# Writing transposed k and q in the order of their blocks, and loading v to match in eight transfers a chunk, in an attention and feed-forward kernel

## The chip, the cores and the metric

The kernel runs on one core of a Trainium2 chip. The time is the device time of one execution in microseconds (us). Several executions are taken, and each is marked fast, slow or unknown; only fast runs are compared. The profile is of one execution, and its span is some 2 us shorter than the time of that execution (564.6 and 566.4 us for the kernel before).

Short names: PE is TensorE (matmuls), PEld its weight loads, DVE is VectorE, ACT is ScalarE, POOL is GpSimd, SP is SyncE, which here only issues transfers, in order. L294 is line 294 of the kernel that the profile belongs to, so the same statement has another number in another kernel. An evacuation is the copy by which another engine takes a finished product away from TensorE. An issue is the instruction that starts a transfer; the transfer lands later.

## The reference, cut

```python
# q, k, v: (4, 8, 768, 48), alpha the same, in 0.8 to 1.0; all fp32
for t in range(S):
    state = alpha[:, :, t, :, None] * state + np.einsum('bhd,bhe->bhde', k[:, :, t], v[:, :, t])
    y[:, :, t] = np.einsum('bhd,bhde->bhe', q[:, :, t], state)
x = y.transpose(0, 2, 1, 3).reshape(3072, 384)
h = x @ w_in                                   # (384, 2048)
g = h * np.clip(h + 3.0, 0.0, 6.0) / 6.0
out = g @ w_out                                # (2048, 384)
```

## The kernel before, as far as the change touches it

The sequence is worked in 24 chunks of 128 tokens; two chunks are one group of 256 rows of the feed-forward part. Chunks 0 to 5 are loaded by token and transposed by TensorE. From chunk 6 on (`FIRST`), alpha, k and q come from DRAM with partition u holding tokens 4u to 4u+3, and VectorE turns them in blocks of 32 by 32. What leaves a block transpose is in the order (v, u), v being the token's place within its four. The kernel before writes it back in token order, each element 16 bytes after the last.

```python
def load_v(j, z):                              # by token, two transfers a chunk
    to = v_t[j].rearrange("s (p a) e -> s p a e", a=2)
    sv = rows(v, j).rearrange("(p a) s d -> s p a d", a=2)
    nc.sync.dma_start(out=to[:, :, 0, 0:D], in_=sv[:, :, 0])
    nc.sync.dma_start(out=to[:, :, 1, 64 - D : 64], in_=sv[:, :, 1])

def by_blocks(to, name, j):                    # k, q and alpha from chunk 6 on
    nc.vector.transpose(out=to.rearrange("r p (u v) -> r p v u", v=V),
                        in_=quads[name, j % NQ][:, :, :, 0:BLK])

def scaled(name, j):                           # k times R, q times P (decays along the chunk)
    ...
    by = R_t[j][:, :, 1:W] if name == "k" else without_first(P_t.pop(j))
    nc.vector.tensor_tensor(out=t, in0=src, in1=by, op=ALU.mult)

def write_k(j):                                # scaled k, turned again, goes to DRAM as far ...
    for o in range(V):
        nc.sync.dma_start(out=to[o], in_=src[BLK * o : BLK * (o + 1)])

def read_k(j):                                 # ... and is read back as kb, by token
    nc.sync.dma_start(out=kb_t[j].rearrange("s p r -> s (p r)"), in_=...)

def update(j):                                 # TensorE: state += kb^T v
    ...
def store2(g, i):                              # a finished quarter of a group's output
    nc.scalar.dma_start(out=out[j * C : (j + 1) * C, col * HD : (col + 1) * HD],
                        in_=oh_t.pop((g, i)))
```

All loads and k's round trip (`far`, then `kb`) are issued by SyncE, one after another; the stores are issued by ScalarE. A hand-made string of words fixes the order of all work on every engine: `lv.6.1` is the load of v for chunk 6, `kw.6` and `kr.6` are the two halves of k's round trip.

## Time and profile before

| | before |
|---|---|
| median of the first runs | 568.94 us (568.49 to 569.09) |
| span of the profiled run | 564.6 us |
| TensorE busy | 553.4 us, 98% |
| VectorE busy | 470.0 us, 83% |

The busy line, the stretches, TensorE's waits and the transposes are in the prediction below. Two views also belong here. The first is the chain of work that ended last, by engine, from the page:

```profile
PE 89%; DMA 6%; DVE 2%; SPq 1%; issue 0%; ACT 0%; DVEq 0%; ACTq 0%
```

The chain runs through TensorE for 89% of the span: that is a kernel bound by TensorE. The second is what SyncE's queue waited for (engine, line, what it waited for: us in all, times, longest us):

```profile
SPq L267 <- DMA out_dram<-oh: 27.7, 13, 4.6
SPq L267 <- DMA kb<-far: 9.0, 4, 3.1
```

L267 is a load of alpha, k or q. It waits, 13 times, for a *store* of results (`out_dram<-oh`), although no buffer connects the two.

### The profile page before, as it was taken

What the parts mean: (1) busy time and instruction counts of PE and PEld (TensorE: products, weight loads), DVE (VectorE), ACT (ScalarE), POOL (GpSimd) and SP (SyncE); (2) the same over time, 40 slices, a digit from 0 to 9 for tenths busy, and PEclk for the clock granted to TensorE, in tenths of its full rate; (3) what the DMA queues carried; (4) which work ended last, traced back from release to release, by engine and by line L of the source; (5) the groups of instructions that cost most, each with busy time, mean ns of one, the idle gap of its engine ahead of it and who ended that gap; (6) DMA issues with size and microseconds to landing.
All of it is one profiled execution on the core that took longest, in us unless ns stands there. A gap on an engine that the chain in (4) does not pass through costs nothing.

```text
span 564.6 us, 12762 instructions
## 1 busy us (share of the span) xinstructions
PE 553.4 (98%) x5236; PEld 513.2 (91%) x5236; DVE 470.0 (83%) x798; ACT 196.4 (35%) x348; POOL 56.0 (10%) x70
## 2 busy tenths in 40 slices
PE   8899999999899999999999999999999999999997
PEld 7688987599799989999999999999999999999997
DVE  7866997999899999998998978976999967754580
ACT  1457664112332332322422422432521422432420
POOL 2333435200001000100000000000000000000000
PEclk9979999999999999999999999999999999999999
DMA  9999677103533636264264353153154340000000
GB/s 147 188 186 168 186 230 196 52 16 63 139 90 87 145 71 155 54 139 90 60 148 107 77 121 85 20 146 78 45 129 94 83 122 8 1 22 8 1 30 21
DMA packets 121272, 53.73 MB, mean 95 GB/s; under 512 B 80638, under 2 KB 114174, under 8 KB 121214
## 3 DMA queue, kind: packets, MB, share of 16 engines
q1 hardware_dynamic: 114588, 48.19, 40.8%
q10 hardware_dynamic: 6624, 4.72, 2.5%
q8 instruction: 41, 0.67, 0.5%
q14 instruction: 19, 0.14, 0.1%
HBM read 44.24 MB, written 8.65 MB: 94 GB/s over the span
## 4 chain that ended last, share of the span: by engine, by line
PE 89%; DMA 6%; DVE 2%; SPq 1%; issue 0%; ACT 0%; DVEq 0%; ACTq 0%
PE m_ps L692 35%; PE m_ps L592 29%; PE m_ps L471 6%; PE sc_ps L346 4%; PE m_ps L509 4%; PE y_ps L440 4%; DMA rings<-in_k_dram 3%; PE y_ps L450 2%; PE m_ps L482 2%; DMA t<-in_v_dram 2%; PE u_ps L410 2%; DMA kb<-far 1%; PE tk_ps L288 1%; DMA far<-kq 1%; PE m_ps L524 0%
## 5 line engine op out<-in xcount | busy, mean ns | idle before, releaser
L692 PE MATMUL m_ps<-w,g_sb 128*128 128x192 f32 x704 | 121.2, 328 | 0.0
L692 PEld LDWEIGHTS m_ps<-w,g_sb 128*128 128x128 f32 x704 | 113.8, 190 | 2.3 <-issue 1.4
L598 ACT COPY g_sb<-m_ps 128x512 f32<-128x512 f32 x110 | 64.3, 584 | 138.3 <-PE m_ps L592 123.9
L692 PE MATMUL m_ps<-rings,g_sb 128*128 128x192 f32 x528 | 91.2, 326 | 0.0
L692 PEld LDWEIGHTS m_ps<-rings,g_sb 128*128 128x128 f32 x528 | 85.7, 190 | 0.0
L592 PE MATMUL m_ps<-xc,w 128*128 128x128 f32 x640 | 83.2, 278 | 0.2 <-ACT g_sb L598 0.2
L592 PEld LDWEIGHTS m_ps<-xc,w 128*128 128x128 f32 x640 | 77.2, 192 | 3.3 <-issue 1.4
L487 ACT ACTIVATE r<-g_sb,half 128x512 f32<-128x512 f32 x80 | 55.5, 719 | 57.0 <-DVE g_sb L529 22.8
L491 DVE SCALAR_TENSOR_TENSOR g_sb<-r,g_sb 128x512 f32<-128x512 f32 x80 | 54.5, 700 | 8.1 <-PE m_ps L692 4.8
L397 POOL TENSOR_TENSOR t<-t,R 128x384 f32<-128x384 f32 x20 | 20.9, 1043 | 383.8 <-DVE t L425 206.0
L592 PE MATMUL m_ps<-xT,raw 128*128 128x128 f32 x400 | 51.8, 276 | 0.0
L592 PEld LDWEIGHTS m_ps<-xT,raw 128*128 128x128 f32 x400 | 48.7, 192 | 0.3
L529 DVE TENSOR_TENSOR g_sb<-m_ps,g_sb 128x512 f32<-128x512 f32 x30 | 20.5, 686 | 27.2 <-ACT g_sb L598 26.5
L592 PE MATMUL m_ps<-xT,w 128*128 128x128 f32 x320 | 41.9, 278 | 0.0
L639 DVE TENSOR_TENSOR g_sb<-g_sb 128x512 f32<-128x512 f32 (+1 forms) x55 | 41.7, 796 | 0.1
L592 PEld LDWEIGHTS m_ps<-xT,w 128*128 128x128 f32 x320 | 38.2, 192 | 1.2 <-issue 0.2
L352 DVE TENSOR_TENSOR A<-sc_ps,mask 128x512 f32<-128x512 f32 x48 | 30.8, 683 | 2.7 <-PE sc_ps L346 2.4
L592 PE MATMUL m_ps<-xc,raw 128*128 128x128 f32 x240 | 32.1, 277 | 0.7 <-ACT g_sb L598 0.7
L471 PE MATMUL m_ps<-xT,w 128*128 128x256 f32 x144 | 32.7, 381 | 0.0
L315 DVE TENSOR_TENSOR_SCAN R<-t,ones 128x516 f32<-128x516 f32 x24 | 29.3, 1223 | 3.1 <-ACT t L306 2.8
L529 DVE TENSOR_TENSOR g_sb<-g_sb 128x512 f32<-128x512 f32 x40 | 27.2, 683 | 5.5 <-ACT g_sb L598 5.4
L592 PEld LDWEIGHTS m_ps<-xc,raw 128*128 128x128 f32 x240 | 29.9, 192 | 1.2 <-ACT g_sb L598 0.9
(110 smaller groups left out, 711.4 us busy)
## 6 DMA issues: line engine op xcount, KB each, us to landing
raw<-in_moe_w_out_dram SPq DMA_DIRECT2D x8, 768.0 KB
t<-in_v_dram SPq DMA_DIRECT2D x48, 96.0 KB
raw<-in_moe_w_in_dram SPq DMA_DIRECT2D x24, 192.0 KB
out_dram<-oh ACTq DMA_DIRECT2D x44, 96.0 KB
far<-kq SPq DMA_DIRECT2D x60, 64.0 KB
kb<-far SPq DMA_DIRECT2D x15, 256.0 KB
kq<-in_k_dram SPq DMA_DIRECT2D x36, 96.0 KB
aq<-in_alpha_dram SPq DMA_DIRECT2D x36, 96.0 KB
```

The lines of the kernel that those rows point to most:

```text
L315: nc.vector.tensor_tensor_scan(out=reverse(R, n - 1, n), data0=reverse(ax, n, n), data1=reverse(ones, n, n), initial=0.0, op0=ALU.mult, op ...
L346: nc.tensor.matmul(sc[h % 2][:, h // 2], K_t[j][r, h // 2], Q_t[j][r, h // 2], start=True, stop=True)
L352: nc.vector.tensor_tensor(out=A_t[j][:, NP * o : NP * (o + 1)], in0=ps_t.pop(("sc%d" % o, j)), in1=mask.unsqueeze(1).to_broadcast([C, NP, ...
L440: nc.tensor.matmul(y_of(j, (i + 1) // 2, p), vs[:, 2 * p + a, 32 * e : 32 * e + 32], A[:, NP * a + p], start=(i % 3 == 0), stop=(i > 1 and ...
L471: nc.tensor.matmul(h[:, f], w1[:, kk, o : o + C], xT_t[g][:, kk], start=(kk == 0), stop=(kk == KT - 1))
L487: nc.scalar.activation(out=to, in_=h, func=AF.Relu, bias=half, scale=1.0 / 6.0)
L491: nc.vector.scalar_tensor_tensor(out=to, in0=r, scalar=1.0, in1=h, op0=ALU.min, op1=ALU.mult)
L529: eng.tensor_tensor(out=out, in0=in0, in1=in1, op=ALU.add if s1 > 0 else ALU.subtract)
L592: nc.tensor.matmul(acc[g][i][:, f * C : (f + 1) * C], spots[w][:, f * C : (f + 1) * C], x_of(g, x), start=(first and f == 0), stop=last, s ...
L598: nc.scalar.copy(out=slots[z], in_=acc[g][i])
L639: nc.vector.tensor_tensor(out=out, in0=in0, in1=in1, op=ALU.subtract)
L692: nc.tensor.matmul(to[g], a, rhs[:, f], start=(first and f == 0), stop=(last and f == HF - 1), skip_group_check=True)
```

## The change

Its intent: let VectorE write k and q in the order (v, u) in which the block transpose produces them, in runs. Then the chunk's tokens stand in that order everywhere, so v is loaded to match, with 32 partitions for each v and half of the heads (eight transfers), the mask is permuted, and the stores undo the order. The schedule string is a new one.

```diff
     def load_v(j, z):
         v_t[j] = ring["v", z]
         to = v_t[j].rearrange("s (p a) e -> s p a e", a=2)
-        sv = rows(v, j).rearrange("(p a) s d -> s p a d", a=2)
-        nc.sync.dma_start(out=to[:, :, 0, 0:D], in_=sv[:, :, 0])
-        nc.sync.dma_start(out=to[:, :, 1, 64 - D : 64], in_=sv[:, :, 1])
+        sv = rows(v, j)
+        if j < FIRST:
+            ... (as before)
+            return
+        sv = sv.rearrange("(p a) (u v) d -> a v u p d", a=2, v=V)
+        for a in range(2):
+            for x in range(V):
+                nc.sync.dma_start(
+                    out=to[BLK * x : BLK * (x + 1), :, a, (64 - D) * a : (64 - D) * a + D],
+                    in_=sv[a, x])
     def by_blocks(to, name, j):
-        nc.vector.transpose(out=to.rearrange("r p (u v) -> r p v u", v=V),
-                            in_=quads[name, j % NQ][:, :, :, 0:BLK])
+        nc.vector.transpose(out=fourth(to) if name == "a" else to.rearrange(
+            "r p (v u) -> r p v u", v=V), in_=quads[name, j % NQ][:, :, :, 0:BLK])
+    def fourth(t):
+        return t.rearrange("r p (u v) -> r p v u", v=V)
     def scaled(name, j):
-        nc.vector.tensor_tensor(out=t, in0=src, in1=by, op=ALU.mult)
+        to = t
+        if j >= FIRST:
+            by = fourth(by)
+            to = src = t.rearrange("r p (v u) -> r p v u", v=V)
+        nc.vector.tensor_tensor(out=to, in0=src, in1=by, op=ALU.mult)
     def store2(g, i):
+        to = out[j * C : (j + 1) * C, col * HD : (col + 1) * HD]
+        if j >= FIRST:
+            to = to.rearrange("(u v) n -> v u n", v=V)
+        nc.scalar.dma_start(out=to, in_=oh_t.pop((g, i)))
     ... (a permuted mask; the schedule string)
```

## The prediction

> **What bounds the kernel now.** I read the page's busy line first, then stretches of the span, then what ended TensorE's waits, then the groups and forms of the transposes and loads.
>
> ```profile
> PE 553.4 (98%) x5236; PEld 513.2 (91%) x5236; DVE 470.0 (83%) x798; ACT 196.4 (35%) x348; POOL 56.0 (10%) x70
> ```
>
> TensorE (PE) is busy for 553.4 of 564.6 us. Busy can hide stretched matmuls, so I asked for the busy time in stretches that I chose by the work in them: start-up, dense layers of the first group, the switch to the later schedule, the steady part, the tail. The first figure after the stretch is its length, then PE, PEld, DVE, ACT, POOL, the granted clock and DMA.
>
> ```profile
> 0.00:30.00 30.00, 25.25 (x268) 21.20 (x269) 22.53 (x41) 10.56 (x16) 9.15 (x25) 0.95 1.18 165
> 30.00:100.00 70.00, 70.00 (x634) 58.46 (x634) 55.52 (x83) 44.25 (x61) 29.31 (x25) 0.97 0.86 195
> 130.00:165.00 35.00, 32.77 (x345) 30.42 (x345) 33.27 (x58) 13.29 (x25) 1.24 (x1) 1.00 0.51 110
> 218.00:240.00 22.00, 20.86 (x243) 19.70 (x242) 21.13 (x34) 8.55 (x15) 2.11 (x2) 1.00 0.38 91
> 240.00:500.00 260.00, 260.00 (x2590) 248.51 (x2589) 223.79 (x393) 84.32 (x163) 9.17 (x10) 1.00 0.37 85
> 500.00:564.60 64.60, 61.54 (x496) 59.98 (x494) 31.93 (x59) 17.78 (x35) 0.00 (x0) 1.00 0.05 16
> ```
>
> All of PE's idle time is here: 4.75 us before 30, 2.23 us in 130 to 165, 1.14 us in 218 to 240, 3.06 us at the end (the last store). Sum 11.2 us. From 240 to 500 PE is never idle. In that part one pair of chunks takes about 43.3 us (260 over six); its own matmuls at their issue rates (162 ns for a 192-wide record of L692, about 112 ns for L592, plus 6.6 us of attention, from the chain of waits) sum to some 43 us. So at most a few tenths of a microsecond per pair are stretched.
>
> ```profile
> PE u_ps L410 <- DMA kb<-far: 2.1, 2, 1.1
> PE tk_ps L288 <- DMA rings<-in_k_dram: 2.0, 2, 1.9
> PE m_ps L592 <- ACT g_sb L598: 0.9, 2, 0.7
> ```
>
> These are PE's own waits: what it waited for, us, times, longest. They name the round trip of k through DRAM (written as far, read back as kb) and chunk 2's k load. VectorE is named for 0.6 us in all.
>
> ```profile
> L292 DVE STREAM_TRANSPOSE q<-qq 128x512 f32<-128x512 f32 x18 | 20.1, 1117 | 0.7 <-DMA qq<-in_q_dram 0.7
> L292 DVE STREAM_TRANSPOSE k<-kq 128x512 f32<-128x512 f32 x18 | 20.1, 1115 | 5.3 <-DMA kq<-in_k_dram 5.3
> L380 DVE STREAM_TRANSPOSE kq<-k 128x512 f32<-128x512 f32 x15 | 10.6, 706 | 0.1
> L338 DVE TENSOR_TENSOR q<-q,P 128x512 f32<-128x512 f32 x18 | 12.4, 686 | 0.1
> L338 DVE TENSOR_TENSOR k<-k,R 128x512 f32<-128x512 f32 x18 | 12.2, 679 | 0.0
> ```
>
> Two transposes of one size cost 1117 and 706 ns. The slow one writes each element 16 bytes after the last (it restores token order), the fast one writes runs. That is what the change goes after.
>
> **What the Trainium skill says.** SBUF — State Buffer, the note on "cachelines" under Door 1: lines of 16 bytes, at least two hits in a line for full bandwidth, and a penalty for each access that crosses to another line. The trace agrees for writes: +411 ns over 512 elements. No row here shows a 16-byte-strided read. VectorE: DVE Perf Modes, "Mode 1×": an fp32 tensor_tensor gives one result a cycle; 512 at the page's 0.96 GHz are 533 ns, plus overhead, against 679 to 686 measured. DMA: Bandwidth & Descriptors, "Rules for kernel authors", advises against many small transfers and says that transfers to disjoint partitions share the same engines; I expect no bandwidth from eight transfers, only issue time. TensorE: Matmul & The Clock Gate, "What's actually happening": idleness brings the half clock. The trace agrees: after the 1.9 us gap at 23.7 us the granted clock is 0.86 in 20 to 30 and 0.79 in 30 to 40.
>
> **The change, part by part.**
> VectorE: 36 transposes (18 each of k and q) drop from about 1116 to about 706 ns, 36 x 0.41 = 14.8 us less. But R and P stay in token order, so the 36 multiplications now read them at 16 bytes. If reads pay as writes do, each grows from 683 to about 1090 ns and takes the 14.8 us back; if not, VectorE falls from 470 to 455 us. I give either even odds. The alpha transpose (1106) and the one back (706) stay. The mask multiplies have the same form, so stay at 683.
> On the path: VectorE idles 36 us in 240 to 500 beside a PE that never idles, so its saving there is worth nothing. It can matter only in 100 to 240, for chunks 6 to 11: 6 x 0.82 = 4.9 us of VectorE, against 3.4 us of PE idle that mostly names a DMA. Worth 0 to 2 us.
> SyncE queue: v was two issues of 497 and 480 ns; now eight like those of k (median 430). So 3.4 for 0.98 us, +2.5 us a chunk, 18 chunks, 44 us of issuing. Each chunk had about 9 us of issuing in 21.7, now about 11.7: it fits. Bytes and 192-byte runs are unchanged.
> Mask: eight small GpSimd copies before the pads, an estimated 2 us at the start (a 128-wide memset there took about 0.2 us), beside the first loads. Stores: same runs, other rows: 0.
> Schedule, start: filler matmuls rise from 28 to 38 (before: 9.5 us for 28, so an estimated +3 us), all before the first dense product. The new order puts the evacuation of chunk 0's k after a weight slice in ScalarE's order, and that slice is the 8th to 11th unit of 196 KB on the queue: 2.2 MB, reached at about 14 us by the 141 and 186 GB/s of the first two 10 us stretches, usable about 16. So chunk 0's update (15.9 before) comes near 18.5. Chunk 2's k moves from the 18th to the 21st unit. The same attention work precedes the first dense product, which began at 29.6 us. I charge +2 us.
> Schedule, middle: before, chunk 6's transpose back began at 132.3 and its k was used at 145.1, so the trip is 12.8 us, with PE waiting 1.1. By the new order, PE work placed between these two is about 11.0, 10.7, 10.7, 10.5 and 11.4 us for chunks 6, 7, 8, 10 and 13 (before: 9.8, 11.9, 13.1, 14.4, 27.0). The shortfalls sum to some 9 us; since words of an order are not times and one wait gives slack to the next, I charge a third, +3 us, and a transpose 0.4 us sooner helps each.
> Credit: the old waits, -3.4 us if all go; I take half, -1.7. A VectorE that gets ahead: -1. Steady part better packed: -2 (0.2 us a pair). Sum +2 +3 -1.7 -1 -2 = +0.3. I put 568.5 us.
>
> **Rivals.** (a) VectorE was the hidden bound, and relief pays in full, 14.8 us: 554. Against: it waits and idles beside a saturated PE. (b) The k round trip and the crowded queue become waits of PE in chunks 6 to 13: for it, the tight new order; against, waits seen so far are 1.1 us each. It would make 574 to 580. (c) A schedule searched anew removes start-up idle, the slow clock (about 3.5 us in 20 to 40) and the middle waits: 558 to 563. (d) Strided reads cost as writes: no VectorE saving, yet only about +1 us, since PE is the bound.
>
> **Range and chances.** 2% faster is 557.6 us, 11.3 us less. That is more than all of PE's idle time including the unavoidable start and last store; matmul work is unchanged. So faster gets 0.03. Slower needs +11.4 us, rival (b) at its full size: 0.05. Same 0.92. Range 560 to 577, from (c) to most of (b).
>
> **What would show it.** k and q transposes near 706 ns (if near 1116, the write explanation is wrong). The multiplications at 683 or at 1090 decide the read. PE busy 550 to 558, with work other than filler near 544. First dense product at 29 to 33 us. Waits of the update for kb above 2 us in total in 130 to 260 show (b). Steady pairs at 43 us. It would be wrong if PE idled in 240 to 500, or if v's last transfer became what an update waits for.

## The result, and the profile after

The kernel after took 582.94 us (median of 4 runs, 581.42 to 584.86), the kernel before 568.72 us in the same rounds. The ratio is 1.0251, with a 95% interval of 1.022 to 1.0283: slower by 2.5%, outside the range that was predicted. Ratios here are the mean time of one kernel's fast runs over the mean of the other's in the same rounds, so they are not quite the ratio of the medians.

The busy line of the page, and below it the chain by engine:

```profile
PE 557.9 (96%) x5256; PEld 514.9 (89%) x5256; DVE 479.3 (83%) x798; ACT 197.3 (34%) x348; POOL 56.7 (10%) x77
...
PE 63%; DVE 17%; DMA 14%; SPq 4%; issue 3%; ACT 0%; DVEq 0%
```

The span grew by 15.0 us (579.6), TensorE's busy time only by 4.5, so its idle time by 10.5 (11.2 to 21.7). DVE, transfers and SyncE's queue now hold 35% of the chain. That share alone proves no loss: in e2 below, whose time is not told from that of the kernel before, they hold 30% (18, 8 and 4). The same stretches as before:

```profile
130.00:165.00 35.00, 34.03 (x366) 31.86 (x365) 34.62 (x62) 13.41 (x25) 0.83 (x1) 1.00 0.45 99
165.00:218.00 53.00, 51.00 (x500) 48.32 (x500) 49.82 (x87) 16.77 (x32) 3.71 (x3) 1.00 0.37 83
218.00:240.00 22.00, 20.58 (x271) 18.29 (x270) 19.16 (x28) 7.35 (x15) 2.92 (x2) 1.00 0.54 123
240.00:500.00 260.00, 252.63 (x2478) 240.25 (x2481) 223.21 (x384) 78.21 (x149) 10.61 (x10) 0.99 0.38 84
```

Between 240 and 500 us TensorE was never idle before. Now it is idle for 7.4 us (260.00 less 252.63), the largest part of the 10.5. What it waited for in the whole span (the same columns as above):

```profile
PE m_ps L620 <- DVE g_sb L557: 3.6, 4, 1.4
PE u_ps L438 <- DMA t<-in_v_dram: 2.8, 1, 2.8
PE u_ps L438 <- DMA kb<-far: 2.0, 2, 1.6
```

By these names it waits for VectorE, for a transfer of v and for k's way back. Two of the names must be followed further. VectorE works in order and itself stands before late loads; between 240 us and the end:

```profile
DVE t L313 <- DMA aq<-in_alpha_dram: 7.0, 3, 2.6
DVE k L313 <- DMA kq<-in_k_dram: 2.4, 2, 1.8
```

That is 9.4 us, against 4.5 in the kernel before. TensorE's longest wait of the first row (1.43 us, at 414.1) comes after three waits of VectorE for loads, of 1.8, 1.9 and 2.6 us, between 398 and 406. So at least a part of "waits for VectorE" is late loads handed on. What the wait for v is will be seen below. VectorE's operations that the change touches:

```profile
L366 DVE TENSOR_TENSOR k<-k,R 128x512 f32<-128x512 f32 x18 | 20.7, 1153 | 0.1
L366 DVE TENSOR_TENSOR q<-q,P 128x512 f32<-128x512 f32 x18 | 20.0, 1112 | 0.1
L313 DVE STREAM_TRANSPOSE k<-kq 128x512 f32<-128x512 f32 x18 | 12.7, 706 | 3.6 <-DMA kq<-in_k_dram 3.5
L313 DVE STREAM_TRANSPOSE q<-qq 128x512 f32<-128x512 f32 x18 | 12.6, 699 | 0.0
```

The transposes fell to 706 and 699 ns as intended; the multiplications, which now read R and P at 16 bytes, rose from 679 and 686 to 1153 and 1112 ns. The saving went straight back. SyncE's queue around the longest of TensorE's waits between 240 and 500, in order of time (start, us, then what was issued and how often):

```profile
247.44 4.29 SPq L277 DMA_DIRECT2D qq<-in_q_dram  x4
251.82 4.03 SPq L294 DMA_DIRECT2D t<-in_v_dram  x8
255.95 2.59 SPq L415 DMA_DIRECT2D far<-kq  x4
260.18 0.56 SPq L419 DMA_DIRECT2D kb<-far  x1
260.84 5.06 SPq L294 DMA_DIRECT2D t<-in_v_dram  x8
```

By the string (`lq.13 lv.12 kw.12 kr.12 lv.13`) this is the round trip of chunk 12's k, and the last row is chunk 13's v. VectorE's two turns of k in this part (ns least, median, most; first and last start), and TensorE's update of chunk 12:

```profile
L408 DVE STREAM_TRANSPOSE kq<-k x2: 699/708/718, 248.9 to 262.6; 128x512 f32<-128x512 f32 x2
265.76 0.88 PE L438 MATMUL u_ps<-t,kb 128*48 128x48 f32 x16 [2.76 <-DMA t<-in_v_dram]
```

VectorE has k ready to be written at 249.6 (248.9 plus 0.7), but the queue is at a load of q, whose fourth transfer waits 2.7 us in it for a store, and then at v's eight until 255.85. The way out starts 6.3 us late, 4.0 of them v's; the way back follows it, and TensorE idles 2.76 us before the update. The profile names v for that wait. By the trace's record of completions it is k: chunk 12's v was in at 257.4, while k's way back was complete at 265.57, just before the update began. So the row of 2.8 us above belongs to k's round trip. A name in that view is an inference and has to be held against the times.

What SyncE waited for:

```profile
SPq L277 <- DMA out_dram<-oh: 35.8, 10, 7.1
SPq L294 <- DMA out_dram<-oh: 13.0, 7, 3.7
```

Its loads now wait 48.8 us (35.8 plus 13.0) for stores, against 28.7 before (the 27.7 above, and 1.0 for v). The sum alone decides nothing: it is 42.2 in e2, which is not told from the kernel before, and 55.4 in f3, which is faster than the kernel after. Why a load waits for a store at all is not in the trace but in the compiled program. These are a few of SyncE's instructions of the kernel after, and two of ScalarE's, with what each waits for:

```
SP   L294 t_93 <- in_v_dram   32x4x48    waits DMAHW3, PE
SP   L294 t_93 <- in_v_dram   32x4x48    waits DMAHW4
SP   L294 t_93 <- in_v_dram   32x4x48    waits DMAHW5
SP   L415 far  <- kq1         512x1x32   waits DMAHW3, DVE
SP   L415 far  <- kq1         512x1x32   waits DMAHW4
ACT  L744 out  <- oh          4x32x192   waits DMAHW1, DVE
ACT  L744 out  <- oh          4x32x192   waits DMAHW4, DVE
```

This program counts the completion of transfers in eight counters, DMAHW0 to DMAHW7, that SyncE's and ScalarE's transfers use in turn. A transfer is issued when the one that had its counter before has landed. So a load whose counter was last used by a store waits for that store, the store waits for a result of VectorE, and everything behind the load waits too. Transfers that GpSimd issues turn in eight counters of their own (DMASW0 to DMASW7).

Three theories went to the chip. **A**: the strided reads make VectorE late. **B**: v's eight transfers crowd SyncE's queue. **C**: the new order of work is itself worse. B was first taken as issue time alone, and had to be split later.

### The profile page after: what moved, and what is told of

It is laid out like the page before. It is cut to its first block, busy times and chain, and to the rows that moved or that the text cites. A ratio compares the mean times of both kernels' runs of the same rounds, so it can differ in the third digit from the quotient of the medians.

```text
span 579.6 us, 12947 instructions
## 1 busy us (share of the span) xinstructions
PE 557.9 (96%) x5256; PEld 514.9 (89%) x5256; DVE 479.3 (83%) x798; ACT 197.3 (34%) x348; POOL 56.7 (10%) x77
## 4 chain that ended last, share of the span: by engine, by line
PE 63%; DVE 17%; DMA 14%; SPq 4%; issue 3%; ACT 0%; DVEq 0%
PE m_ps L720 22%; PE m_ps L620 20%; PE m_ps L499 5%; PE m_ps L537 4%; DMA kb<-far 3%; PE y_ps L468 3%; PE sc_ps L374 3%; DMA kq<-in_k_dram 2%; DMA rings<-in_k_dram 2%; PE m_ps L510 2%; DMA out_dram<-oh 2%; DVE g_sb L667 2%; PE y_ps L478 2%; DMA rings<-in_alpha_dram 2%; DVE P L350 1%
## 5 line engine op out<-in xcount | busy, mean ns | idle before, releaser
L515 ACT ACTIVATE r<-g_sb,half 128x512 f32<-128x512 f32 x80 | 57.3, 722 | 99.8 <-DVE g_sb L557 36.7
L620 PE MATMUL m_ps<-xc,w 128*128 128x128 f32 x640 | 84.4, 279 | 3.7 <-DVE g_sb L557 3.6
L425 POOL TENSOR_TENSOR t<-t,R 128x384 f32<-128x384 f32 x20 | 22.4, 1119 | 383.0 <-DVE t L453 240.7
L620 PE MATMUL m_ps<-xT,raw 128*128 128x128 f32 x400 | 54.1, 281 | 0.0
L620 PEld LDWEIGHTS m_ps<-xT,raw 128*128 128x128 f32 x400 | 49.9, 194 | 1.2 <-issue 0.4
L339 DVE TENSOR_TENSOR_SCAN R<-t,ones 128x516 f32<-128x516 f32 x24 | 31.2, 1300 | 2.0 <-ACT t L330 1.4
```

The source lines that it names most:

```text
L339: nc.vector.tensor_tensor_scan(out=reverse(R, n - 1, n), data0=reverse(ax, n, n), data1=reverse(ones, n, n), initial=0.0, op0=ALU.mult, op ...
L425: nc.gpsimd.tensor_tensor(out=st[j % 2], in0=sm[j % 2], in1=R_t[j][:, :, 0:1].to_broadcast([C, NP, 2 * D]), op=ALU.mult)
L515: nc.scalar.activation(out=to, in_=h, func=AF.Relu, bias=half, scale=1.0 / 6.0)
L620: nc.tensor.matmul(acc[g][i][:, f * C : (f + 1) * C], spots[w][:, f * C : (f + 1) * C], x_of(g, x), start=(first and f == 0), stop=last, s ...
```

## The experiments

| run | kernel | median us | ratio to before, 95% interval |
|---|---|---|---|
| after | after | 582.9 | 1.0251 (1.022 to 1.0283) |
| e1 | after, order of before | 609.8 | 1.0707 (1.0624 to 1.0789) |
| e2 | before, order of after | 571.5 | 1.0047 (0.9986 to 1.0107) |
| e3 | after, reads in runs (wrong result) | 582.7 | 1.0237 (1.0169 to 1.0304) |
| e4 | after, v in two (wrong result) | 574.6 | 1.0091 (1.0024 to 1.0158) |
| e5 | e3 and e4 together (wrong result) | 570.0 | 1.0041 (1.0 to 1.0082) |
| f1 | before, v in eight | 596.6 | 1.0521 (1.0446 to 1.0595) |
| f5 | after, v in four | 579.9 | 1.0224 (1.0163 to 1.0284) |
| f3 | after, v's eight by GpSimd | 574.5 | 1.012 (1.0062 to 1.0178) |
| g2 | after, v's eight by ScalarE | 605.7 | 1.0662 (1.0608 to 1.0717) |
| g7 | f3 in the order of before | 575.2 | 1.012 (1.0067 to 1.0172) |
| h1 | after, stores by GpSimd | 575.5 | 1.0089 (1.0035 to 1.0144) |
| h4 | f1, stores by GpSimd | 581.9 | 1.0236 (1.0177 to 1.0294) |
| f6 | before, v in one | 566.9 | 0.9982 (0.9917 to 1.0047) |
| g3 | before, v's two by GpSimd | 567.4 | 1.0004 (0.996 to 1.0047) |
| h2 | before, stores by GpSimd | 567.7 | 0.9966 (0.9926 to 1.0006) |
| h5 | f6, stores by GpSimd | 568.8 | 0.9994 (0.9944 to 1.0045) |

The kernel before took 567.1 to 569.8 us (medians) on different chips; the ratios compare better than the medians. Results are correct except where the table says that they are wrong on purpose.

### e1 and e2: layout and order, each alone

```diff
-        run("""la.1 z.3.5 lq.1 la.0 ...          (e1: the kernel after)
+        run("""la.0 z.3.5 lq.0 lk.0 ...          (with the string of before)
```

> The changed kernel with the order of the kernel before; correct result. Theory A (VectorE runs late: the new order was made for multiplications of 683 ns, and they take about 1130, 0.9 us more a chunk): the old order was made for the same VectorE sum (1116 + 683 against 706 + 1130 ns), so 568 to 572 us. Theory B (the eight issues of v hold up the SyncE queue, in any order): 573 to 582 us. Theory C (the new order is simply worse): 568 to 572 us, as A.

```diff
-        run("""la.0 z.3.5 lq.0 lk.0 ...          (e2: the kernel before)
+        run("""la.1 z.3.5 lq.1 la.0 ...          (with the string of after)
```

> The kernel before with the order of the changed one: v in two transfers, k and q in token order, VectorE sum per chunk as in the changed kernel to 0.1 us; correct result. A: 580 to 584 us, VectorE is as late as in the changed kernel. B: 569 to 575 us, v is cheap again. C: 580 to 584 us.

The new order on the old layout cost 0.5%, not told from nothing. The old order on the new layout took 609.8 us. So theory C falls: by e2's interval the new order is worth 1.1% at most, and on the new layout it saves some 26 us (1.0707 to 1.0251). None of the three theories had foreseen the size of e1; B, the nearest, said 573 to 582 us. SyncE's queue in e1, for chunk 6, and TensorE's update of that chunk:

```profile
131.27 3.75 SPq L415 DMA_DIRECT2D far<-kq  x4
135.12 4.85 SPq L294 DMA_DIRECT2D t<-in_v_dram  x8
140.01 0.65 SPq L419 DMA_DIRECT2D kb<-far  x1
```

```profile
147.34 1.08 PE L438 MATMUL u_ps<-t,kb 128*48 128x48 f32 x16 [5.04 <-issue]
```

v's eight stand between the two halves of k's round trip for 4.85 us, and TensorE is idle for 5.04 us before the update. In the kernel before, two issues of v stood in this place, and the same update had this wait:

```profile
145.09 0.56 PE L410 MATMUL u_ps<-t,kb 128*48 128x48 f32 x16 [1.14 <-DMA kb<-far]
```

### e3, e4 and e5: the reads, the eight transfers, and both

```diff
 e3, e5:
-            by = fourth(by)
+            by = by.rearrange("r p (v u) -> r p v u", v=V)
 e4, e5 (in load_v):
-        if j < FIRST:
+        if True:
```

In e3 the multiplication reads R and P in runs and so takes the wrong elements; in e4 v is loaded by token while k and q are not. The amount of work is the same, the results are wrong.

> The changed kernel, but the 36 multiplications read R and P in runs (wrong result on purpose: factors of other tokens); VectorE 36 x 0.45 = 16 us less. The multiplications fall to about 685 ns. A: 567 to 573 us, PE's waits for VectorE (3.6 us and more) go. B and C: 579 us or more, since PE's waits for v and kb stay.

> The changed kernel, but v of the later chunks in two transfers, in token order (wrong result on purpose: v rows do not match k and the scores). A and C: 580 to 584 us. B: 569 to 575 us, and PE's one wait of 2.8 us for v goes.

> The changed kernel with v in two transfers and multiplications that read in runs (wrong result on purpose), VectorE 16 us less than with v in two alone (574.6). If the strided reads cost time once the queue is free: 568 to 572 us, the time of the old layout in the new order (571.5) or less. If not: 573 to 576 us.

e3's multiplications fell as the theory asks:

```profile
L366 DVE TENSOR_TENSOR k<-k,R 128x512 f32<-128x512 f32 x18 | 13.2, 739 | 0.1
L366 DVE TENSOR_TENSOR q<-q,P 128x512 f32<-128x512 f32 x18 | 12.7, 705 | 0.1
```

They gave VectorE 14.8 us back (20.7 and 20.0 less 13.2 and 12.7), and the time did not move: 582.7. Theory A falls as the cause. e4 left the reads alone and recovered 8.3 us (582.9 to 574.6). With the transfers out of the way, the reads may show: e5 is 4.6 us below e4 by the medians, 2.8 by the ratios. The two ran in different calls and their intervals overlap, so this is not shown.

### f1, f5 and f3: how many transfers, and whose

f1 puts only the eight transfers into the kernel before, by token, with nothing else changed.

```diff
 f1 (the kernel before, chunks from 6 on):
-        nc.sync.dma_start(out=to[:, :, 0, 0:D], in_=sv[:, :, 0])
-        nc.sync.dma_start(out=to[:, :, 1, 64 - D : 64], in_=sv[:, :, 1])
+        for a in range(2):
+            for x in range(V):
+                r = slice(BLK * x, BLK * (x + 1))
+                nc.sync.dma_start(out=to[r, :, a, (64 - D) * a : (64 - D) * a + D], in_=sv[r, :, a])
```

> The kernel before, untouched in layout and order, but v of the later chunks in eight transfers of 32 partitions in token order: the same bytes, runs and places; correct result. Theory B (eight issues of about 0.45 us on SyncE, in front of the loads and of the k round trip): 595 to 612 us, that is most of what the new layout with the old order lost (609.8). Rival D (the block layout, with its multiplications of 1076 ns, was a large part of that loss): 569 to 585 us.

```diff
 f5 (the kernel after; the heads of v lie 80 elements apart, so that one transfer serves both halves):
-        for a in range(2):
-            for x in range(V):
-                nc.sync.dma_start(out=to[BLK * x : BLK * (x + 1), :, a, ...], in_=sv[a, x])
+        for x in range(V):
+            nc.sync.dma_start(out=to[BLK * x : BLK * (x + 1)], in_=sv[x])
```

> The changed kernel with v's heads at a uniform pitch of 80, so that a block of v comes in one transfer and a chunk in four; correct result. B: between two (574.6) and eight (583), by the number of issues 576 to 579 us. If issues did not matter but the blocks of 32 partitions did, 581 to 584 us.

```diff
 f3 (the kernel after):
-                nc.sync.dma_start(
+                nc.gpsimd.dma_start(
```

> The changed kernel with the same eight transfers of v, issued by GpSimd's queue instead of SyncE's; correct result. B: the transfers themselves cost nothing, so 572 to 577 us, as with two. If the transfers of 32 partitions are slow in themselves: 581 us or more. If GpSimd's issuing is slow, its decayed state comes late and PE's y waits: over 583 us.

f1 is the cleanest proof of B: eight transfers in place of two, and the kernel before takes 29 us more. Of the 28.3 us by which its span is longer (592.9), TensorE is idle for 22.0 (33.2 against 11.2); the other 6.3 it is busy for longer with the same 5236 instructions, and its granted clock between 130 and 240 us was 0.90 to 0.94, against 1.00 before. Its loads do not wait longer for stores in all, but elsewhere: with k's two ways the waits for stores are 33.3 us here and 33.4 before, and most of them now stand at v's own line, where they were 1.0.

```profile
SPq L283 <- DMA out_dram<-oh: 27.0, 15, 3.8
```

f3 keeps every transfer, its bytes and its 32 partitions, and only issues it from GpSimd: 574.5 us, the same as with two transfers (e4). So the transfers themselves cost nothing that shows; it is their place in SyncE's queue, or among its counters, which f3 changes too. Four transfers (f5) took 579.9 us, between what had been expected for issues (576 to 579) and for blocks (581 to 584); its interval overlaps those of eight and of two, so it is told from neither.

### g2 and g7: v by ScalarE, and the old order with a free queue

```diff
 g2 (the kernel after):
-                nc.sync.dma_start(
+                nc.scalar.dma_start(
```

> The changed kernel, v's eight transfers issued by ScalarE's queue; correct result. They still take turns in the same eight completion counters as SyncE's transfers and the stores. If SyncE's issue time alone is the cause: 573 to 578 us. If the shared counters are (a transfer waits for the one eight before it): 581 us or more; a ScalarE that waits in order for v's buffers would also show so, in PE's waits for ScalarE.

```diff
 g7 (f3):
-        run("""la.1 z.3.5 lq.1 la.0 ...
+        run("""la.0 z.3.5 lq.0 lk.0 ...          (the string of before)
```

> The changed layout with the old order, which lost 42 us (609.8), but v's eight transfers issued by GpSimd; correct result. If the crowded SyncE queue was the whole of that loss: 566 to 572 us. If the strided reads hurt in the old order: 575 us or more.

g2 was meant to free SyncE, and cannot be read so. ScalarE works in order too and also has evacuations to do. What waited in it:

```profile
ACT g_sb L626 <- DMA t<-in_v_dram: 24.1, 6, 6.1
PE m_ps L620 <- ACT g_sb L626: 13.1, 6, 3.6
SPq L277 <- DMA t<-in_v_dram: 41.2, 27, 6.5
```

ScalarE's evacuations stood 24.1 us behind v's transfers, TensorE waited 13.1 us for the evacuations, and SyncE still waited for v, since both use the same eight counters. That last row was the hint that the counters matter.

g7 against e1 is the change of queue in the old order: 609.8 to 575.2 us. Its steady stretch is full again:

```profile
240.00:500.00 260.00, 260.00 (x2591) 248.52 (x2590) 228.57 (x398) 85.38 (x165) 56.39 (x97) 1.00 0.37 84
```

TensorE is never idle there although the strided reads are all in it. In the old order they cost nothing in that stretch, as the prediction said of VectorE's time. The run as a whole fell on the edge of the case in which they do hurt (575 or more had been expected for it); more under what stays open.

### h1 and h4: the stores off the shared counters

If issue time alone made the queue too long, then leaving v's eight issues on SyncE must keep the loss. If the waits for stores make it, then moving only the stores to GpSimd, whose transfers use other counters, must take it away.

```diff
 h1 (the kernel after; h4 makes the same edit in f1):
-        nc.scalar.dma_start(out=to, in_=oh_t.pop((g, i)))
+        nc.gpsimd.dma_start(out=to, in_=oh_t.pop((g, i)))
```

> The changed kernel with its 44 stores issued by GpSimd instead of ScalarE; correct result. If loads that wait in SyncE's queue for a store's counter are the cause: 571 to 577 us, and SyncE's waits for out (about 50 us) go. If the issue time is: 580 to 584 us, with those waits gone all the same.

> The kernel before with v of the later chunks in eight transfers on SyncE (that alone took 596.6 us, +29 us), and the result stores given to GpSimd's queue, so that they no longer take turns with the loads in the eight completion counters. Counters theory: the loads no longer wait in order for a store that waits for a result, so the +29 us go almost wholly: 568 to 575 us, SyncE waits for out_dram near 0. Issue-time theory: the eight issues are as many and as long (about 430 ns each) as before, so most stays: 585 to 597 us.

h1 took 575.5 us, as e4 and f3 did, with all eight issues still in SyncE's queue. So in the new order issue time alone is not the cause: it costs the 7 to 9 us only together with the stores where they were. Its stretch, and the start of the way out of chunk 12's k, which VectorE had ready at 249.2:

```profile
240.00:500.00 260.00, 257.73 (x2543) 245.73 (x2541) 228.58 (x390) 81.22 (x155) 27.26 (x34) 1.00 0.39 83
249.21 2.62 SPq L415 DMA_DIRECT2D far<-kq  x4
```

TensorE's idle time there fell from 7.4 to 2.3 us. No load waits for a store any more; the only such row left is the end of the program (L928). The way out starts at once, where it was 6.3 us late in the kernel after (4.3 in e4, 2.3 in f3), and the update that idled 2.76 us there idles 0 (1.1 in e4, 0 in f3).

A rival remains: the edit also takes the stores out of ScalarE's order, and in the kernel after ScalarE stood 11.9 us behind its own stores. The trace speaks against it, since TensorE waits for ScalarE 0.2 us there and 0.4 in h1 (4.8 in f1 and 5.2 in h4, which makes the same edit), and e4 and f3 are as fast with the stores still on ScalarE; no run separates the two.

h4 met neither expectation: 581.9 us, half of f1's loss gone and half left. The stretch from 240 to 500 recovered (TensorE's idle time is 1.9 us, in f1 10.9). In the whole span TensorE is idle for 23.4 us (578.2 less 554.8 busy), against 11.2 before. Of these 12.2 us more, 6.0 lie from 130 to 240, where the later chunks begin; 2.5 are at the end, 1.9 in the steady stretch, and 1.8 ahead of 30 us, where the two kernels do the same (g3, on another chip, has 1.4 of them too). SyncE's queue of h4 for chunk 6:

```profile
134.21 3.93 SPq L283 DMA_DIRECT2D t<-in_v_dram  x8
138.18 0.64 SPq L397 DMA_DIRECT2D kb<-far  x1
```

```profile
145.00 0.91 PE L416 MATMUL u_ps<-t,kb 128*48 128x48 f32 x16 [3.81 <-issue]
```

No store is near; v's eight issues alone stand before k's way back for 3.93 us. Not all of that is delay, since the way out has to land first: in g7, where v is in another queue, the way back starts 1.6 us after the last issue of the way out has ended (134.82 to 136.46), here 4.1 us after it (134.11 to 138.18). So v delays it by about 2.4 us, in e1 by 3.4. TensorE idles 3.81 us before the update; in the kernel before it idled 1.1 us here. In the old order, then, the issue time itself is a cost too, because v stands inside k's round trip. That the stores matter as well shows on VectorE: it waits 35.3 us for loads of k and alpha in f1, 17.8 in h4. How the other gains and losses of h4 divide between issue time and the rest was not measured.

### f6, g3, h2 and h5: is there anything to gain in the kernel before?

```diff
 f6: v in one transfer a chunk (heads 80 elements apart)
+        nc.sync.dma_start(out=to, in_=rows(v, j).rearrange("h s d -> s h d"))
 g3: v's two transfers by GpSimd from chunk 6 on
+        eng = nc.sync if j < FIRST else nc.gpsimd
 h2: the stores by GpSimd
-        nc.scalar.dma_start(out=out[...], ...)
+        nc.gpsimd.dma_start(out=out[...], ...)
 h5: f6 and h2 together
```

> The kernel before with v at a pitch of 80 and one transfer a chunk, 24 issues fewer; correct result. B: 564 to 568 us, a little under before, since one issue less (0.5 us a chunk) stands before the k round trip, where PE waited 1.1 us twice. Else the same as before, 567 to 569 us.

> The kernel before, v's two transfers of the later chunks issued by GpSimd; correct result. SyncE is relieved of 36 issues (17 us): at best PE's two waits for kb (2.1 us) go, 564 to 567 us; if the queue is not what bounds the old kernel, no change within 0.5%.

> The kernel before with its 44 stores issued by GpSimd; correct result. PE idles only 11 us there, of which some 3 us wait for loads: 565 to 569 us by either account; below 564 only if the stores' counters held up the start of the later schedule.

> The kernel before with v in one transfer a chunk (566.9 us by itself, ratio 0.998) and the stores given to GpSimd's queue (567.7 us by itself, ratio 0.997): the candidate to beat both kernels. If SyncE's queue costs the kernel before anything, both reliefs together should show it: 561 to 565 us. If TensorE alone bounds it (553.4 us busy and 11 us of idle outside the middle), it stays at 565 to 569 us.

All four are the same as the kernel before. In it the queue's waits for stores (27.7 us) cost nothing that shows (h2). No version was found that beats both kernels. One transfer for both halves of v in the block order, and scans that write R and P in block order, could not be built (too many dimensions for a transfer, and for a scan), so a layout without both costs was not tried.

## Why the prediction was wrong, point by point

**The bound.** Right for the kernel before: TensorE was never idle in the steady part. It did not stay so, and the prediction had named this as what would prove it wrong.

**VectorE.** The transposes came out as predicted (706 and 699 ns). Reads at 16 bytes cost what writes do (1076 to 1153 ns in the runs), one of the two cases given even odds. That this is worth little was right in its cause (e3: 14.8 us back on VectorE, nothing in time). Rival (d) put it at about 1 us; beside a free queue it may be 3 to 5 us (e4 to e5), with overlapping intervals.

**SyncE's queue: the step that failed.** The prediction said "Each chunk had about 9 us of issuing in 21.7, now about 11.7: it fits", and charged nothing. The count was right: v's issues have a median of 430 ns, and 430 times eight is 3.4 us. Two things were wrong with it.

First, a queue that fits on average can still be late. What stands behind v in the order is a half of k's round trip, and it is late: in the kernel after, chunk 12's way out by 6.3 us, 4.0 of them v's issues; in the old order, chunk 6's way back by 3.4 us (e1) and 2.4 us (h4). The page DMA: Bandwidth & Descriptors of the Trainium skill says in "Anatomy of one DMA" that a semaphore wait happens on the issuing sequencer, before dispatch. The traces agree: in the kernel after the fourth load of q waits 2.7 us for a store and starts at 251.4, and v's and k's issues stand behind it, at 251.8 and 255.95.

Second, issue time is not all that a queue spends. I added the rows of SyncE's timeline from 240 to 500 us, waits inside a row of several issues included. The sum is 127 us before, 184 us after, 178 us in f1 and 155 us in h4. Of the 52 us between f1 and before, h4 takes away 23 without removing an issue; the same move in the kernel before (h2) takes away 2. So in f1 the stores cost SyncE time that they do not cost before, although the waits for them, added up, are as long (33.3 and 33.4 us): they have moved to v, in front of k's way back. That the place is what makes them cost is argued from these rows; no run tests it alone.

The term that was charged 0 measures 29 us in the old order (f1) and 7 to 9 us in the new (e4, f3, h1). About half of the 29 goes when the stores leave the shared counters (h4); in the new order removing either the issues (e4, f3) or the waits for stores (h1) takes the 7 to 9 us away.

A wait for a store is not a loss by itself. e4's loads of alpha, k and q wait for stores as long as those of the kernel after (33.8 us against 35.8), f3's longer (55.4), and both are faster. What counts is whether something on k's way to TensorE is behind the wait.

**The rivals.** Rival (b), "The k round trip and the crowded queue become waits of PE", is what happened, but placed half wrongly. It was held to chunks 6 to 13 and to the new order, and put at 574 to 580 us. Of the 7.4 us between 240 and 500, 3.2 are at the updates of chunks 12 and 13 (2.76 and 0.46) and the rest comes later; and the new order is what limits the loss (e1). The first sign that would prove the prediction wrong, TensorE idle between 240 and 500, came; the second, an update that waits for v, is there by the profile's name alone.

**The schedule.** Start-up, charged +2 us: the first dense product began at 29.96 us, against 29.55 before, so +0.4. Middle: TensorE's idle time from 130 to 165 fell from 2.2 to 1.0 us, while 165 to 218 lost 2.0. The credit of 2 us for a better packed steady part did not come: e2, with no layout change, is idle for 1.9 us there. The sum of these terms near zero agrees with e2 (+0.5%, not told from nothing), but by terms that were off and cancelled: that is luck. Also, +0.3 on the 568.9 us before gives 569.2, not the 568.5 that was put; nothing hangs on it.

**What stays open.** With the queue freed, the new layout still costs about 1%: g7 (1.012) against g3 (1.0004), which have v on GpSimd and the old order in common, and whose intervals do not overlap. The strided reads may be one part of that; no run shows their size. In g7 another may be that TensorE waits 2.9 us for v by the profile's names, which comes through GpSimd. The split was not measured further. The two scans also take longer in the new order, with either layout: 1223 and 1218 ns before, 1269 and 1246 in e2, 1222 and 1219 in g7. Why is not known; 24 of each make some 2 us of VectorE. The plainest test of the place in the queue was not run: the same eight issues of v, moved behind both halves of k's round trip in the string.

## What to carry to other kernels

Count a change of loads as places in an in-order queue, not as issue time or bytes: look at which transfer on the critical round trip stands behind the added ones, and by how much it moves. Read what the issuing queue waits for; a load that waits for a store that shares no buffer with it is a sign of shared completion counters, and moving one of the two to another issuing engine is a one-word test. Hold the name that a view gives to a wait against the times before building on it. When a reordering makes a write contiguous, ask who now reads against the order; here the cost only changed instructions.

## What the Trainium skill lacked or had wrong

- DMA: Bandwidth & Descriptors, "Issuing engines are not separate DMA queues", says that starting transfers from several engines will only save the sequencer's time to initiate them. Here more was at stake than initiation: moving only the stores from ScalarE to GpSimd left SyncE's issues as they were and took 7 us (582.9 to 575.5); as read here, because it took the stores off the completion counters that loads wait on.
- No page says that in such a program SyncE's and ScalarE's transfers take turns in eight completion counters, so that a load waits for an unrelated store (28.7 us of its loads' waits before, 48.8 us after), nor that GpSimd's use eight others. This is a fact of the compiled program rather than of the chip.
- DMA: Bandwidth & Descriptors, "Rules for kernel authors", advises one transfer in place of many small ones. The advice was right here (two to eight: 29 us in f1), but not for the overhead that it names: the same eight small transfers cost nothing that shows from another queue (f3 574.5 us, e4 with two 574.6).
- SBUF — State Buffer, the note on cachelines under Door 1, held for reads as for writes: reads at 16 bytes 1076 to 1153 ns against 679 to 686 in runs, writes 1117 against 706. It gives no figure for the penalty; here it is some 0.4 us over 512 fp32 elements.
